# Expert stage of an attention and mixture-of-experts kernel: a three-armed Switch replaced by fp32 units of 64 tokens in nested conditions

## The chip, the cores and the metric

The kernel runs on one core of a Trainium2 chip. The metric is device time in microseconds (us). The engines are TensorE (PE in the profile; its weight loads are PEld), VectorE (DVE), ScalarE (ACT), GpSimd (POOL) and SyncE (SP), which here issues DMAs. Each engine has its own instruction stream with its own branches.

## The reference

Attention with queries pooled by two, then a top-1 mixture of experts with a fixed capacity. Shapes: 2 batches, 8 heads, 1152 positions, head dimension 64; pooled queries make N = 1152 tokens of D = 512. There are 8 experts with F = 1024 and a capacity of 288 tokens; tokens beyond the capacity are dropped and their rows stay zero.

```python
q_pool = q.reshape(B, H, S // 2, 2, 64).mean(axis=3)
attn = softmax(q_pool @ k.T / 8)
x = (attn @ v) as (1152, 512)                  # tokens
expert_idx = argmax(x @ w_gate); gate_w = its softmax probability
disp[e, pos] = x[i]                            # at most 288 tokens of each expert, in order
h = maximum(einsum('ecd,edf->ecf', disp, w1), 0)
y = einsum('ecf,efd->ecd', h, w2)
out[i] = gate_w[i] * y[expert_idx[i], pos[i]]  # 0 for dropped tokens
```

Inputs, outputs and all results are fp32. With the inputs used, the experts get 27, 61, 69, 288 (374 before the cut), 51, 63, 267 and 240 tokens.

## The kernel before

The first part computes attention and the routes of the tokens, and writes each token's row with its gate and its row numbers into a DRAM buffer `xs`, sorted by expert, 288 rows for each. `classes()` turns the counts per expert into class numbers, and each engine loads the eight class numbers into registers (L1027). Eight products that nobody reads (`warm`, L697) keep TensorE running meanwhile. The change leaves all this alone but for `classes()`.

The expert stage starts at about 350 us. For each expert in turn there is a `tc.Switch` on its class (L1039) with one arm per class, written out as straight code in each of the eight Switches. Classes are: no token, up to 32, up to 64, up to 128, up to 256, up to 288 tokens. There are three kinds of arms:

- "columns" (`by_columns`, up to 64 tokens) works in plain fp32. The tokens, transposed, are the stationary operand and the raw weights stream past in pieces of 256 columns. A group of 64 tokens fills half of TensorE's columns, so two groups stand side by side, each with its half of F. First product L834, relu on ScalarE (L841) for the first half of columns and on VectorE (L839) for the second, transposes back (`turn`, L846), copies (ScalarE L851, VectorE L849), second product L869, gate factor and copy `yo` (L799), send by an indirect DMA on GpSimd (L805).
- "tokens" (`by_tokens`, up to 128) and "weights" (`by_weights`, up to 256 or 288) split every operand into two float32r parts and add three products. The weights are split in the arm: ScalarE casts (L738) and VectorE subtracts (L740). First products are L907 and L939, second ones L917 and L975, and L961 for the last 32 tokens of 288.

In this run experts 0 to 7 take the arms for 32, 64, 128, 288, 64, 64, 288 and 256. Weights come in chunks of 1 MB, four for an expert, into eight buffers `wraw`; six chunks are loaded during attention, and a chunk that is done with starts the load of the chunk eight later. Each arm also loads the tokens of the expert after the next (SyncE), transposes the first 128 tokens of the next (`trans_x0`, L768, with its copy `xf` at L770) and splits those and the next expert's first weight chunk.

The order of instructions on SyncE, ScalarE, VectorE and TensorE is that of the text (`manual_schedule`); GpSimd's is set by the scheduler. At the end of an arm each engine leaves the Switch (rows at L1062, in which registers are set) and goes to the arm of the next one (from L1062 to L1039).

Of the kernel before, what the change touches and what calls it, by code (L numbers as in the profile page):

```python
# [23 lines left out]
NR, NR0 = 8, 6  # L24
FAR = 1.0e6
ALT = 2
# [8 lines left out]
def attention_moe(ctx: ExitStack, tc, cap, q, k, v, wg, w1, w2, out):  # L35
    nc = tc.nc
# [56 lines left out]
    NG0 = cap if cap <= 288 else 2 * P  # L93
    sizes = sorted({n for n in (D // 2, D, P, 2 * P, cap) if n <= cap})
    arms = [(-1, 0, "none")]
    for n in sizes:
        arms.append((arms[-1][1], n, "columns" if n in (D // 2, D) else "tokens" if n <= P else "weights"))
    cls_i = const.tile([P, E], I32, name="cls_i")
# [6 lines left out]
    # tokens of each expert so far on each partition: small whole numbers, exact in float32r  # L105
# [52 lines left out]
    # the small terms of the mixed tile: high parts of both heads' keys, low parts of both heads' queries  # L158
# [100 lines left out]
    def prep_first():  # L259
        # nothing runs beside the first pair's operands: split straight out of PSUM  # L260
# [136 lines left out]
    # query groups of a second product: (group of P^T, columns, token tiles and their rows)  # L397
# [134 lines left out]
    def classes():  # L532
        ps = m_ps.tile([P, 512], F32, tag="t", name="cps")
        nc.tensor.matmul(ps[:, 0:E], ones, totals[0][:, 0], start=True, stop=True)
        cl = xp.tile([P, 2, E], F32, tag="cl", name="cl")
        c, g = cl[:, 0], cl[:, 1]
        for i, (lo, _, _) in enumerate(arms[1:]):
            d = c if i == 0 else g
            nc.vector.tensor_scalar(out=d, in0=ps[:, 0:E], scalar1=lo + 0.5, scalar2=None, op0=ALU.is_ge)
            if i:  # L540
                nc.vector.tensor_tensor(out=c, in0=c, in1=g, op=ALU.add)
        return nc.vector.tensor_copy(cls_i, c)

    # filled before the tokens are placed: slots without a token hold zeros and a token beyond the last
# [49 lines left out]
    with ExitStack():  # L594
# [12 lines left out]
        # the last pair: its products, outputs and routes as soon as each group of queries is through  # L607
# [85 lines left out]
        # the tensor engine halves its clock when it idles for long: products that nobody reads keep it up  # L693
        # while the last tokens are placed
# [7 lines left out]
    # up to 64 tokens go through float32 passes in two column groups; more go through three passes of  # L702
    # operands split into two float32r parts each
    NM = NG0 + NG0 % 2
    XB = (NG0 + P - 1) // P
    N0 = min(P, NG0)
    h_p = ctx.enter_context(tc.tile_pool(name="hp", reuse_waits="tile", bufs=1))
    y_p = ctx.enter_context(tc.tile_pool(name="yp", reuse_waits="tile", bufs=2))
# [5 lines left out]

    hh = h_p.tile([P, FC, NM], F32R, name="hh")
    hl = h_p.tile([P, FC, NM], F32R, name="hl")
    hs = h_p.tile([P, 2, 512], F32, name="hs")
    ht = h_p.tile([P, 4, P], F32, name="ht")
    hr = h_p.tile([P, FC, D], F32, name="hr")
    whs = [ws_p.tile([P, 4, 512], F32R, name=f"wh{i}") for i in range(4)]  # L720
    wls = [ws_p.tile([P, 4, 512], F32R, name=f"wl{i}") for i in range(4)]
    xes = [xe_p.tile([P, XB, ROW], F32, name=f"xe{i}") for i in range(2)]
    gts = [xe_p.tile([P, XB + 3], F32, name=f"gt{i}") for i in range(4)]
    ids = [xe_p.tile([P, XB + 3], I32, name=f"id{i}") for i in range(4)]
    xfs = [xe_p.tile([P, DC, N0], F32, name=f"xf{i}") for i in range(2)]
    xhs = [xe_p.tile([P, DC, NM], F32R, name=f"xh{i}") for i in range(2)]
    xls = [xe_p.tile([P, DC, NM], F32R, name=f"xl{i}") for i in range(2)]
    wraw += [ws_p.tile([P, 4, 512], F32, name=f"wraw{i}") for i in range(NR0, NR)]
    if NM > NG0:
        for t in xhs + xls:  # L730
            nc.vector.memset(f32(t[:, :, NG0:NM]), 0.0)

    def split_w(i, a, alt=False):
        r, h, lo = wraw[i % NR], whs[i % 4], wls[i % 4]
        if alt:
            nc.vector.tensor_copy(h[:, a], r[:, a])
        else:
            nc.scalar.copy(h[:, a], r[:, a])  # L738
        eng = nc.gpsimd if alt else nc.vector
        eng.tensor_tensor(out=lo[:, a], in0=r[:, a], in1=f32(h[:, a]), op=ALU.subtract)  # L740

    def blocks(n):
        return [(s, min(P, n - s)) for s in range(0, n, P)]

    def load_x(e, o, n, b0, b1):
        for s, c in blocks(n)[b0:b1]:
            r = e * cap + o + s
            nc.sync.dma_start(out=xes[e % 2][0:c, s // P, :], in_=xs[r:r + c, :])

    def tags(e, b, c):  # L750
        xe, gt, it = xes[e % 2], gts[e % 4], ids[e % 4]
        nc.gpsimd.tensor_copy(gt[0:c, b:b + 1], xe[0:c, b, DM:DM + 1])  # L752
        nc.gpsimd.tensor_copy(it[0:c, b:b + 1], xe[0:c, b, DM + 1:DM + 2].bitcast(I32))
        if b == 0:
            sides = [(XB + i, w) for i, w in ((0, D), (2, D // 2)) if w <= c]
        else:
            sides = [(XB + 1, c)] if c in (D // 2, D) else []
        for col, w in sides:
            for g in range(2):
                rows = slice(g * w, (g + 1) * w)  # L760
                nc.gpsimd.tensor_copy(gt[rows, col:col + 1], xe[0:w, b, DM:DM + 1])
                nc.gpsimd.tensor_copy(it[rows, col:col + 1], xe[0:w, b, DM + 2 + g:DM + 3 + g].bitcast(I32))

    def trans_x0(e):
        xe, xf = xes[e % 2], xfs[e % 2]
        ps = tr_ps.tile([P, 512], F32, tag="tr", name="xps")
        for d in range(DC):
            nc.tensor.transpose(ps[:, d * N0:(d + 1) * N0], xe[0:N0, 0, d * P:(d + 1) * P], ident[0:N0, 0:N0])  # L768
        tags(e, 0, N0)
        nc.scalar.copy(xf, ps[:, 0:DC * N0].rearrange("p (d c) -> p d c", c=N0))  # L770

    def split_x0(e):
        xf, xh, xl = xfs[e % 2], xhs[e % 2], xls[e % 2]
        nc.scalar.copy(xh[:, :, 0:N0], xf)
        nc.vector.tensor_tensor(out=xl[:, :, 0:N0], in0=xf, in1=f32(xh[:, :, 0:N0]), op=ALU.subtract)

    def trans_x(e, n, first):
        xe, xh, xl = xes[e % 2], xhs[e % 2], xls[e % 2]
        bl = blocks(n)[first:]
        if not bl:  # L780
            return
        s0 = bl[0][0]
        for d in range(DC):
            ps = (h_ps if d == 3 else tr_ps).tile([P, 512], F32, tag="h" if d == 3 else "tr", name="xps")
            for s, c in bl:
                nc.tensor.transpose(ps[:, s:s + c], xe[0:c, s // P, d * P:(d + 1) * P], ident[0:c, 0:c])
            nc.scalar.copy(xh[:, d, s0:n], ps[:, s0:n])  # L787
            nc.vector.tensor_tensor(
                out=xl[:, d, s0:n], in0=ps[:, s0:n], in1=f32(xh[:, d, s0:n]), op=ALU.subtract
            )  # L790
        for s, c in bl:
            tags(e, s // P, c)

    def send(e, b, c, ps, halves=1, part=None):
        n = DM // halves
        gate = gts[e % 4][0:c, b:b + 1]
        yo = y_p.tile([P, DM], F32, tag="yo", name="yo", bufs=4)
        if part is None:
            nc.scalar.activation(yo[0:c, 0:n], ps[0:c, 0:n], AF.Copy, scale=gate)  # L799
        else:  # L800
            yq = y_p.tile([D, n], F32, tag="yq", name="yq", bufs=1)
            nc.scalar.copy(yq[0:c], ps[part:part + c, 0:n])
            nc.vector.tensor_tensor(out=yq[0:c], in0=ps[0:c, 0:n], in1=yq[0:c], op=ALU.add)
            nc.vector.tensor_scalar(out=yo[0:c, 0:n], in0=yq[0:c], scalar1=gate, scalar2=None, op0=ALU.mult)
        ins = nc.gpsimd.indirect_dma_start(  # L805
            out=out.rearrange("t (g d) -> (t g) d", g=halves),
            out_offset=bass.IndirectOffsetOnAxis(ap=ids[e % 4][0:c, b:b + 1], axis=0),
            in_=yo[0:c, 0:n],
            in_offset=None,
            bounds_check=NTOK * halves - 1,  # L810
            oob_is_err=False,
        ).ins
        tc.declare_no_dep(ins, group="send", reason="each token has a row of its own")
        tc.add_to_no_dep_group("send", ins)

    def load_next(i):
        if i + NR < 4 * E:
            load_w(i + NR)

    def by_columns(e, n, step):  # L820
        xf = xfs[e % 2]
        c0 = 4 * e
        raw = [wraw[(c0 + c) % NR] for c in range(4)]
        G = P // n
        Q = F // G // 256

        def up(q):
# [10 lines left out]
            if q:  # L838
                nc.vector.tensor_scalar_max(hs[:, q, 0:256], ps[:, 0:256], 0.0)  # L839
            else:  # L840
                nc.scalar.activation(hs[:, q, 0:256], ps[:, 0:256], AF.Relu)  # L841
# [224 lines left out]
```

## Time and profile before

| | us |
|---|---|
| median of three runs | 570.49 (569.73 to 574.44) |
| span of the profiled execution | 565.9 |
| TensorE busy in it | 468.0 (83%) |
| VectorE, ScalarE, GpSimd busy | 330.8, 296.5, 164.1 |
| mean granted TensorE clock | 0.917 of full speed |

The profiled execution has no time of its own beside its span. The span, from the first to the last instruction, is 4.6 us below the median of the runs, which also hold the start and the end around it. Times below count from the start of the span.

In the chain of waits, a piece belongs to the engine and line that ran, and "issue" is time in which an engine waited for nothing that the profile shows; names such as ACTq are an engine's sequencer with registers and branches. TensorE's fp32 products leave two records each. DMA share is the mean busy share of the core's 16 DMA engines.

### The profile page before, as it was taken

What the parts mean: (1) busy time and instruction counts of PE and PEld (TensorE: products, weight loads), DVE (VectorE), ACT (ScalarE), POOL (GpSimd) and SP (SyncE); (2) the same over time, 40 slices, a digit from 0 to 9 for tenths busy, and PEclk for the clock granted to TensorE, in tenths of its full rate; (3) what the DMA queues carried; (4) which work ended last, traced back from release to release, by engine and by line L of the source; (5) the groups of instructions that cost most, each with busy time, mean ns of one, the idle gap of its engine ahead of it and who ended that gap; (6) DMA issues with size and microseconds to landing.
All of it is one profiled execution on the core that took longest, in us unless ns stands there. A gap on an engine that the chain in (4) does not pass through costs nothing.

```text
span 565.9 us, 8678 instructions
## 1 busy us (share of the span) xinstructions
PE 468.0 (83%) x2809; PEld 328.8 (58%) x2809; DVE 330.8 (58%) x837; ACT 296.5 (52%) x840; POOL 164.1 (29%) x303
## 2 busy tenths in 40 slices
PE   4889989989989989999999987465839965569794
PEld 3657757656656656666676753233529732368693
DVE  6697886785878976876875663202637320237160
ACT  5767766657657647666766640211527330236250
POOL 4574450351442652432410012110321221011101
PEclk9799999999999989999999997767878996769898
DMA  8899932311321421320120006869745566900101
GB/s 245 188 298 374 351 91 48 83 49 43 83 75 53 120 65 38 83 46 2 43 47 1 1 37 199 273 203 314 236 147 173 178 213 192 324 18 4 45 2 38
DMA packets 56790, 71.11 MB, mean 126 GB/s; under 512 B 21794, under 2 KB 32036, under 8 KB 56608
## 3 DMA queue, kind: packets, MB, share of 16 engines
q1 hardware_dynamic: 52672, 57.72, 33.9%
q0 software_dynamic: 3392, 11.50, 5.7%
q14 instruction: 135, 1.11, 0.9%
q8 instruction: 47, 0.77, 0.6%
q10 hardware_dynamic: 544, 0.02, 0.1%
HBM read 52.48 MB, written 11.92 MB: 114 GB/s over the span
## 4 chain that ended last, share of the span: by engine, by line
PE 59%; DVE 18%; issue 15%; ACT 5%; DMA 1%; another core or an unknown queue 1%; ACTq 0%; SPq 0%; POOL 0%; POOLq 0%; DVEq 0%
PE s L346 13%; PE pv L409 13%; PE tp L384 10%; PE hps L939 8%; DVE q L243 7%; DVE negm L351 5%; PE yps L975 5%; PE warm L697 2%; PE xps L439 2%; ACT wh L738 2%; DVE pt L393 2%; PE hps L834 1%; ACT p L367 1%; PE kps L195 1%
## 5 line engine op out<-in xcount | busy, mean ns | idle before, releaser
L351 DVE TENSOR_REDUCE negm<-s 128x1 f32<-128x384 f32 x216 | 115.8, 553 | 63.6 <-PE s L346 60.4
L367 ACT ACTIVATE p<-s,negm 128x384 f32<-128x384 f32 x216 | 124.4, 582 | 38.3 <-DVE negm L355 32.8
L346 PE MATMUL s<-k,q 128*128 128x384 f32 x432 | 127.7, 387 | 9.8 <-ACT p L367 9.8
L384 PE MATMUL tp<-ident,p 128*128 128x128 f32 x648 | 108.6, 280 | 7.5 <-DVE pt L393 7.5
L409 PE MATMUL pv<-pt,vraw 128*64 128x256 f32 (+2 forms) x612 | 106.9, 406 | 0.0
L395 ACT COPY pt<-tp 128x384 f32<-128x384 f32 (+1 forms) x160 | 70.0, 453 | 50.8 <-PE tp L384 49.8
L346 PEld LDWEIGHTS s<-k,q 128*128 128x128 f32 x432 | 68.1, 195 | 48.4 <-ACT p L367 32.8
L384 PEld LDWEIGHTS tp<-ident,p 128*128 128x128 f32 x648 | 80.5, 142 | 24.2 <-DVE pt L393 11.9
L409 PEld LDWEIGHTS pv<-pt,vraw 128*64 128x64 f32 x612 | 41.8, 136 | 33.8 <-issue 19.2
L206 POOL TENSOR_TENSOR k<-kts,k 64x384 fp32r<-64x384 f32 x42 | 42.2, 1005 | 65.7 <-DVE k L205 40.4
L740 DVE TENSOR_TENSOR wl<-wraw,wh 128x512 fp32r<-128x512 f32 x78 | 50.0, 685 | 14.5 <-ACT wh L738 13.4
L249 POOL TENSOR_TENSOR q<-qts,q 64x256 fp32r<-64x256 f32 (+1 forms) x76 | 50.8, 676 | 17.2 <-DVE q L243 9.4
L738 ACT CAST wh<-wraw 128x512 fp32r<-128x512 f32 x78 | 44.0, 619 | 12.7 <-issue 12.7
L805 POOL DMA_INDIRECT out_dram<-yo,id x13 | 15.9, 1224 | 101.0 <-ACT yo L799 55.0
L393 DVE COPY pt<-tp 128x384 f32<-128x384 f32 (+1 forms) x80 | 40.2, 511 | 6.8 <-PE tp L384 6.0
L367 ACT ACTIVATION_READ_ACCUMULATOR p<-s,negm 128x1 f32 x216 | 43.8, 203 | 0.0
L243 DVE CAST q<-qts 64x256 fp32r<-64x256 f32 (+1 forms) x70 | 42.2, 617 | 1.1
L834 PE MATMUL hps<-wraw,xf 128*64 128x256 f32 (+1 forms) x128 | 20.8, 544 | 21.1 <-issue 21.1
L839 DVE TENSOR_SCALAR hs<-hps 128x256 f32<-128x256 f32 x3 | 1.3, 425 | 46.7 <-PE hps L834 46.7
L834 PEld LDWEIGHTS hps<-wraw,xf 128*64 128x64 f32 (+1 forms) x128 | 11.3, 182 | 28.8 <-issue 28.1
L939 PE MATMUL hps<-xh,wh 128*128 128x288 f32 (+1 forms) x96 | 19.4, 330 | 8.4 <-ACT xh L787 8.4
L752 POOL COPY gt<-xe 128x1 f32<-128x1 f32 (+1 forms) x13 | 2.4, 183 | 74.9 <-issue 65.3
(157 smaller groups left out, 583.9 us busy)
## 6 DMA issues: line engine op xcount, KB each, us to landing
wraw<-in_moe_w_dram SPq DMA_DIRECT2D x32, 1024.0 KB, 8.6
vraw<-in_v_dram SPq DMA_DIRECT2D x8, 576.0 KB, 4.0
kc<-k SPq DMA_DIRECT2D x16, 288.0 KB, 3.8
xs<-zrow POOLq DMA_DIRECT2D x4, 1032.0 KB, 7.0
xe<-xs SPq DMA_DIRECT2D x16, 258.0 KB, 3.6
qraw<-in_q_dram SPq DMA_DIRECT2D x16, 256.0 KB, 3.5
kraw<-in_k_dram SPq DMA_DIRECT2D x14, 288.0 KB, 4.3
out_dram<-zrow POOLq DMA_DIRECT2D x2, 1024.0 KB
```

The source lines that it names most:

```text
L243: nc.vector.tensor_copy(tl[r0, 0, c], qt_s[rs, a:z])
L249: nc.gpsimd.tensor_tensor(out=tl[r0, 1, c], in0=qt_s[rs, a:z], in1=f32(tl[rs, 0, c]), op=ALU.subtract)
L346: nc.tensor.matmul(ps[:, 0:CW], a, w, start=i == 0, stop=i == len(terms) - 1)
L351: nc.vector.tensor_reduce(out=negm3[g][:, j:j + 1], in_=ps[:, 0:CW], axis=AX.X, op=ALU.max, negate=True)
L367: nc.scalar.activation(pexp[g][:, j * CW:(j + 1) * CW], sthird.pop(n)[:, 0:CW], AF.Exp, bias=negm3[g][:, 3:4], scale=1.0, accum_out=sums[p ...
L384: nc.tensor.transpose(ps[:, i * P:(i + 1) * P], pexp[g][:, kt * P:(kt + 1) * P], ident)
L393: nc.vector.tensor_copy(dst, sr)
L395: nc.scalar.copy(dst, sr)
L409: nc.tensor.matmul(ps[j * D:(j + 1) * D, 0:n], vraw[:, j, kt, :], pts[p, j, src][:, kt, c0:c0 + n], start=kt == 0, stop=kt == KT - 1,)
L738: nc.scalar.copy(h[:, a], r[:, a])
L740: eng.tensor_tensor(out=lo[:, a], in0=r[:, a], in1=f32(h[:, a]), op=ALU.subtract)
L939: nc.tensor.matmul(ps[:, 0:ne], a[:, d, fo:fo + P], x[:, d, 0:ne], start=i == 0, stop=i == 3 * DC - 1)
```

## The change

Every expert is worked off in units: tokens 0 to 63, 64 to 127, 128 to 191, 192 to 255 in units of 64, and 256 to 287 in a unit of 32. Each unit is the "columns" arm of before, applied to its tokens. Unit 0 stands in straight code. Unit 1 stands in a condition on a flag, unit 2 in a condition inside unit 1's, and so on, so that every expert has four nested conditions. The flags (`more_i`) are loaded into registers on every engine ahead of each expert's unit 0 (L853), and each unit begins with a hint on the condition that follows. The split operands and their arms are gone. `wraw` has 16 buffers instead of eight, and the load of chunk i + 16 stands behind the nested conditions. The token buffers `xes` are three instead of two, and all blocks of an expert's tokens are transposed on TensorE and copied by ScalarE.

```diff
-NR, NR0 = 8, 6
+NR, NR0 = 16, 6
+NX = 3
...
+    units = []
+    while sum(n for _, n in units) < cap:
+        o = sum(n for _, n in units)
+        units.append((o, D // 2 if cap - o <= D // 2 else D))
+    NU = len(units)
...
-    def by_columns(e, n, step):
+    def unit(e, u, between=()):
+        o, n = units[u]
         xf = xfs[e % 2]
...
                     nc.tensor.matmul(
-                        ps[g * n:(g + 1) * n, 0:256], xf[:, d, 0:n], raw[o // 512][:, d, o % 512:o % 512 + 256],
+                        ps[g * n:(g + 1) * n, 0:256], xf[:, d, o:o + n], raw[c // 512][:, d, c % 512:c % 512 + 256],
                         start=d == 0, stop=d == DC - 1,
                     )
...
+    def later(e, u, flags):
+
+        label = f"u{e}_{u}"
+        with tc.If(flags[u - 1] > 0, preferred_fallthrough_block=True, label=label):
+            if u + 1 < NU:
+                tc.mark_branch_hint_location(f"u{e}_{u + 1}", hint=flags[u], engines=ENG)
+            nxt = units[u + 1][0] if u + 1 < NU else 0
+            unit(e, u, [lambda: trans_x(e, nxt // P)] if nxt and nxt % P == 0 else ())
+            if u + 1 < NU:
+                later(e, u + 1, flags)
...
     with tc.manual_schedule(engines=MS):
-        load_x(0, 0, NG0, 0, XB)
-        load_x(1, 0, NG0, 0, XB)
-        for i in range(NR0, NR):
+        for e in range(min(NX, E)):
+            load_x(e)
+        for i in range(NR0, min(NR, 4 * E)):
             load_w(i)
-        with tc.issue_after(routed):
-            for a in range(4):
-                split_w(0, a)
-        trans_x0(0)
-        split_x0(0)
+        trans_x(0, 0)
         for e in range(E):
-            for i in tc.Switch(cv[e], len(arms)):
-                arm(e, *arms[i][1:])
+            _, flags = nc.values_load_multi_w_load_instructions(more_i[0:1, e, :], min_val=0, max_val=1)
+            tc.mark_branch_hint_location(f"u{e}_1", hint=flags[0], engines=ENG)
+            unit(e, 0, [lambda: trans_x(e + 1, 0)] if e + 1 < E else ())
+            later(e, 1, flags)
+            if e + NX < E:
+                load_x(e + NX)
+            for i in range(4 * e + NR, min(4 * e + NR + 4, 4 * E)):
+                load_w(i)
```

On ScalarE before, expert 4's arm for 64 tokens reads as follows; L1062 is the way out of the arm, L841 the relu, L770 the copy of the next expert's tokens, L738 the casts of the next expert's first chunk:

```order
L1039 BRANCH_PREFETCH_HINT
L841 ACTIVATE hs<-hps 128x256
L851 COPY ht<-htp 128x256
L770 COPY xf_4046<-xps 128x512
L774 CAST xh_4048<-xf_4046 128x4x128
L738 CAST wh_4027<-wraw_154 128x512 x4
L799 ACTIVATE yo<-yps,gt_4037 128x256
L1062 UNCONDITIONAL_BRANCH
```

On ScalarE after, from the end of expert 4's fourth unit over its unit of 32 to the end of expert 5's unit 0 (L795 is the relu, L752 and L755 make yo, L853 loads the flags):

```order
L752 ACTIVATE yo<-yps,gt_4034 128x256
L838 COMPARE_AND_BRANCH
L795 ACTIVATE hs<-hps 128x256
L755 COPY yq<-yps 64x256
L838 UNCONDITIONAL_BRANCH x8
L853 TENSOR_LOAD more_i
L882 BRANCH_PREFETCH_HINT
L795 ACTIVATE hs<-hps 128x256
L805 COPY ht<-htp 128x256
L735 COPY xf_4032<-xps 128x4x128
L752 ACTIVATE yo<-yps,gt_4035 128x256
L838 COMPARE_AND_BRANCH
```

The casts are gone, and eight branches, two for each of the four conditions, stand between an expert's last unit and the next expert's load of flags.

On GpSimd before, the last expert's arm for 288 tokens ends with these rows (L761 and L762 copy gates and row numbers, L805 sends):

```order
L762 COPY id_4044<-xe_4036 32x1
L761 COPY gt_4040<-xe_4036 32x1
L762 COPY id_4044<-xe_4036 32x1
L805 DMA out_dram<-yo,id_4044 2304x256
L805 DMA out_dram<-yo,id_4044 1152x512 x2
L1062 UNCONDITIONAL_BRANCH
L1062 ISA
```

On GpSimd after, the last expert's unit of 32 and what follows it (L743 and L744 copy gates and row numbers, L758 sends; an ISA row here is a wait):

```order
L743 COPY gt_4037<-xe_4030 32x1
L744 COPY id_4041<-xe_4030 32x1
L758 DMA out_dram<-yo,id_4041 2304x256
L838 UNCONDITIONAL_BRANCH
L838 ISA
L838 UNCONDITIONAL_BRANCH
L758 DMA out_dram<-yo,id_4041 2304x256
L838 UNCONDITIONAL_BRANCH
L838 ISA
L838 UNCONDITIONAL_BRANCH
L758 DMA out_dram<-yo,id_4041 2304x256
L838 UNCONDITIONAL_BRANCH
```

The unit of 32 sends inside its condition; the sends of units 3, 2 and 1 stand behind it in that order, each at the end of its own condition, with branches between them.

More of the change, by code (lines that the diff above doesn't have):

```diff
@@ L91, in attention_moe @@
         )
[L93 to L98, printed above, removed]
+    units = []
[3 more added lines that the diff above has]
+    NU = len(units)
+    CT = units[-1][0] + units[-1][1]
+    more_i = const.tile([P, E, NU - 1], I32, name="more_i")
     x_ctx = ExitStack()
@@ L534, in classes @@
         nc.tensor.matmul(ps[:, 0:E], ones, totals[0][:, 0], start=True, stop=True)
[L535 to L542, printed above, removed]
+        cl = xp.tile([P, E, NU - 1], F32, name="cl")
+        for i, (o, _) in enumerate(units[1:]):
+            nc.vector.tensor_scalar(out=cl[:, :, i], in0=ps[:, 0:E], scalar1=o + 0.5, scalar2=None, op0=ALU.is_ge)
+        return nc.vector.tensor_copy(more_i, cl)
     nz = 4
@@ L729, in attention_moe @@
[L729 to L762, printed above, removed]
@@ L764, in trans_x0 @@
-    def trans_x0(e):
-        xe, xf = xes[e % 2], xfs[e % 2]
+    wraw += [ws_p.tile([P, 4, 512], F32, name=f"wraw{i}") for i in range(NR0, NR)]
+    xes = [xe_p.tile([P, XB, ROW], F32, name=f"xe{i}") for i in range(NX)]
+    xfs = [xe_p.tile([P, DC, XB * P], F32, name=f"xf{i}") for i in range(2)]
+    gts = [xe_p.tile([P, NU], F32, name=f"gt{i}") for i in range(4)]
+    ids = [xe_p.tile([P, NU], I32, name=f"id{i}") for i in range(4)]
+    blocks = [(s, min(P, cap - s)) for s in range(0, cap, P)]
@@ L766, in trans_x0, with load_x, trans_x @@
+    for t in xes:
+        if blocks[-1][1] < P and CT > cap:
+            nc.vector.memset(t[:, XB - 1], 0.0)
+    def load_x(e):
+        for s, c in blocks:
+            r = e * cap + s
+            nc.sync.dma_start(out=xes[e % NX][0:c, s // P, :], in_=xs[r:r + c, :])
+    def trans_x(e, b):
+        xe, xf = xes[e % NX], xfs[e % 2]
+        c = blocks[b][1]
         ps = tr_ps.tile([P, 512], F32, tag="tr", name="xps")
         for d in range(DC):
-            nc.tensor.transpose(ps[:, d * N0:(d + 1) * N0], xe[0:N0, 0, d * P:(d + 1) * P], ident[0:N0, 0:N0])
@@ L769, in trans_x0 @@
[L769 to L799, printed above, removed]
-        else:
[L801 to L804, printed above, removed]
+            nc.tensor.transpose(ps[:, d * c:(d + 1) * c], xe[0:c, b, d * P:(d + 1) * P], ident[0:c, 0:c])
@@ new lines, in trans_x, with tags @@
+        nc.scalar.copy(xf[:, :, b * P:b * P + c], ps[:, 0:DC * c].rearrange("p (d c) -> p d c", c=c))
+    def tags(e, u):
+        o, n = units[u]
+        xe, gt, it = xes[e % NX], gts[e % 4], ids[e % 4]
+        src, b = slice(o % P, o % P + n), o // P
+        for g in range(2):
+            rows = slice(g * n, (g + 1) * n)
+            nc.gpsimd.tensor_copy(gt[rows, u:u + 1], xe[src, b, DM:DM + 1])
+            nc.gpsimd.tensor_copy(it[rows, u:u + 1], xe[src, b, DM + 2 + g:DM + 3 + g].bitcast(I32))
@@ new lines, in send @@
+    def send(e, u, ps):
+        n = units[u][1]
+        c = 2 * n
+        gate = gts[e % 4][0:c, u:u + 1]
+        yo = y_p.tile([P, 256], F32, tag="yo", name="yo")
+        if n == D:
+            nc.scalar.activation(yo[0:c], ps[0:c, 0:256], AF.Copy, scale=gate)
+        else:
+            yq = y_p.tile([D, 256], F32, tag="yq", name="yq", bufs=1)
+            nc.scalar.copy(yq[0:c], ps[c:2 * c, 0:256])
+            nc.vector.tensor_tensor(out=yq[0:c], in0=ps[0:c, 0:256], in1=yq[0:c], op=ALU.add)
+            nc.vector.tensor_scalar(out=yo[0:c], in0=yq[0:c], scalar1=gate, scalar2=None, op0=ALU.mult)
@@ L814, in send, with step @@
         tc.add_to_no_dep_group("send", ins)
-    def load_next(i):
-        if i + NR < 4 * E:
-            load_w(i + NR)
-    def by_columns(e, n, step):
+    def unit(e, u, between=()):
+        o, n = units[u]
         xf = xfs[e % 2]
-        c0 = 4 * e
-        raw = [wraw[(c0 + c) % NR] for c in range(4)]
+        raw = [wraw[(4 * e + c) % NR] for c in range(4)]
         G = P // n
         Q = F // G // 256
+        todo = list(between)
+        def step():
+            if todo:
+                todo.pop(0)()
         def up(q):
@@ L863, in by_columns @@
         for i in range(NF):
-            for u in range(U):
-                j, g = divmod(i, 2) if U == 1 else (i % 2, 2 * u + i // 2)
+            for w in range(U):
+                j, g = divmod(i, 2) if U == 1 else (i % 2, 2 * w + i // 2)
                 r = g * (F // G) + j * P
                 for c in range(2):
-                    o = (2 * u + c) * n
+                    k = (2 * w + c) * n
                     nc.tensor.matmul(
-                        ps[o:o + n, 0:256], ht[:, j, g * n:(g + 1) * n],
+                        ps[k:k + n, 0:256], ht[:, j, g * n:(g + 1) * n],
                         raw[2 + r // 512][:, r % 512 // P, c * 256:(c + 1) * 256],
@@ L1027, in attention_moe @@
-    _, cv = nc.values_load_multi_w_load_instructions(cls_i[0:1, :], min_val=0, max_val=len(arms) - 1)
+            if i > 1:
+                step()
+        while todo:
+            step()
+        send(e, u, ps)
+    def later(e, u, flags):
[7 more added lines that the diff above has]
+                later(e, u + 1, flags)
```

180 lines of the change are left out of this document (13 added, 167 removed).

## The prediction

> **What bounds the kernel now.** I read the page first, then the chain of waits from 350 us on, a table of the expert stage cut at the experts' ends, and TensorE's order of time in one expert. The page:
>
> ```profile
> span 565.9 us, 8678 instructions
> ...
> PE 59%; DVE 18%; issue 15%; ACT 5%; DMA 1%; another core or an unknown queue 1%; ACTq 0%; SPq 0%; POOL 0%; POOLq 0%; DVEq 0%
> ...
> L805 POOL DMA_INDIRECT out_dram<-yo,id x13 | 15.9, 1224 | 101.0 <-ACT yo L799 55.0
> ```
>
> Over the span the chain is TensorE. The change touches only the stage after 350 us, and there the shares are others (the columns of the table: window and length in us, each engine's busy us, TensorE's granted clock, DMA share, GB/s):
>
> ```profile
> by line: issue 36.6%; PE hps L939 19.8%; PE yps L975 13.8%; ACT wh L738 4.1%; PE hps L834 3.3%; another core or an unknown queue 2.6%; PE xps L768 1.9%; PE hps L907 1.8%; PE yps L961 1.7%; PE yps L869 1.5%; PE yps L917 1.3%; DMA wraw<-in_mo
> ...
> 350.00:364.00 14.00, 6.49 (x72) 3.13 (x70) 3.55 (x7) 5.23 (x10) 1.42 (x10) 0.76 0.85 280
> 364.00:386.00 22.00, 13.10 (x72) 7.03 (x72) 4.45 (x10) 4.05 (x9) 2.34 (x11) 0.69 0.75 245
> 386.00:413.00 27.00, 17.36 (x62) 12.45 (x60) 12.15 (x18) 11.41 (x22) 7.54 (x13) 0.81 0.77 256
> 413.00:453.00 40.00, 30.83 (x188) 26.09 (x188) 17.44 (x35) 16.00 (x42) 7.30 (x21) 0.87 0.51 165
> 453.00:465.00 12.00, 8.97 (x72) 5.38 (x72) 3.52 (x7) 4.35 (x10) 2.39 (x11) 1.00 0.56 190
> 465.00:487.00 22.00, 12.70 (x72) 7.12 (x72) 3.93 (x8) 4.59 (x10) 2.41 (x11) 0.77 0.73 236
> 487.00:530.00 43.00, 32.06 (x188) 27.32 (x188) 15.91 (x32) 15.75 (x42) 6.78 (x21) 0.80 0.25 80
> 530.00:566.00 36.00, 24.95 (x148) 22.27 (x148) 11.42 (x24) 11.38 (x27) 3.25 (x5) 0.88 0.07 25
> sum 216.00, PE 146.46 PEld 110.79 DVE 72.37 ACT 72.77 POOL 33.44; mean PE 18.31 PEld 13.85 DVE 9.05 ACT 9.10 POOL 4.18
> ```
>
> Of 216 us TensorE works 146; the largest single item of the chain is "issue", time in which an engine waited for nothing that the profile shows. Where it lies, in order of time (start, length, what):
>
> ```profile
> 350.24 0.59 ACT xf L770
> ...
> 352.21 4.03 issue
> 356.24 3.38 PE hps L834 x32
> ...
> 386.17 5.89 issue
> 392.07 0.03 ACTq L1062
> ...
> 392.28 6.75 issue
> 399.03 0.03 ACTq L1039
> ...
> 440.91 11.34 PE yps L975 x48
> ...
> 452.39 0.37 issue
> ...
> 452.97 4.58 issue
> ...
> 470.75 7.28 issue
> 478.03 0.03 ACTq L1039
> ...
> 478.49 0.39 ACT hs L841
> ...
> 486.63 0.06 ACT yo L799
> ...
> 529.96 2.84 issue
> ...
> 559.72 0.42 POOL out_dram L805
> ```
>
> The long pieces stand just behind the last operation of an arm (L1062, the way out) and between L1062 and L1039 (the way into the next arm). So each jump to code that the engine does not hold costs ScalarE some 6 to 7 us while the DMA engines carry 236 to 256 GB/s (386.17, 392.28, 470.75), and 2.84 us at 529.96, where they are all but idle (25 GB/s). Where the last arm runs on into what stands right behind it, it costs 0.37 us (452.39). TensorE does not wait so long on the way out, but it then waits for ScalarE's relu.
>
> [...]
>
> **The change part by part.** Units run: experts 0, 1, 4, 5 one of 64; expert 2 two; 3 and 6 four and one of 32; 7 four.
>
> *Price of a unit.* Expert 4 (51 tokens) takes it already, at clock 1.00 (start, length, engine, line, idle before):
>
> ```profile
> 454.05 2.81 PE L834 MATMUL hps<-wraw,xf 128*64 128x256 f32 x24 [1.81 <-issue]
> 458.45 0.44 PE L846 MATMUL htp<-ident,hs 128*128 128x128 f32 x2 [1.58 <-ACT hs L841]
> ...
> 459.83 0.66 PE L768 MATMUL xps<-ident,xe 128*128 128x128 f32 x4
> ...
> 461.80 2.81 PE L869 MATMUL yps<-wraw,ht 128*64 128x256 f32 x24
> ```
>
> From 458.45 to 464.61 is 6.2 us, of which 0.6 are the next block's transposes; with the first 24 records (2.6 up to their last start) a unit is 8.0 us, 8.6 with transposes. Units 1 to 3 in a row: 3 x 8.0 + 2 x 0.6 = 25.2. The unit of 32 has half the records, but its relu, turn and copy stand uncovered: 5.0 (estimate, from 3.38 for its first product in expert 0 and the chain's short pieces).
>
> Against that, expert 3 took 452.3 - 424.0 = 28.2 us with float32r; now 8.6 + 25.2 + 5.0 = 38.8. Expert 6 loses the same 10.6, expert 7 (24.95 us of TensorE in its row, now 33.8) some 9. Expert 2 gains: 17.4 us become 16.6, and its waits for wh (L738) go. All splits leave ScalarE and VectorE; they lie beside TensorE, so that is worth nothing in experts 3, 6 and 7.
>
> *Entry.* Unit 0 of expert 0 needs no jump: it starts after xf, at 351 instead of 356.24. With the clock at 0.76 in that window it takes 10: its products end at 361 (before: 363.2).
>
> *One jump, unit 1 skipped.* After yo, ScalarE jumps once, where before it jumped out and in. Then it loads the flags and sets registers; the nearest rows are the load of L1027 and the arm's register steps:
>
> ```profile
> L1027 ACTq TENSOR_LOAD <-cls_i x1: 750/750/750, 350.9 to 350.9; - x1
> L1062 PEldq COMPARE_BRANCH  x16: 311/2844/7427, 349.0 to 553.2; - x16
> ```
>
> That is 0.75 + 0.4, say 1.2 us (between 0.4, if the load went out early, and 1.6). From relu to yo is 8.1 us at the lowered clock (478.49 to 486.63), 6.7 at full clock. So from the end of a unit to that of the next: 5.9 + 1.2 + 6.7 to 8.1, say 14.0 with DMA busy, and 2.9 + 1.2 + 6.7 = 11.0 with DMA idle. I take busy for experts 0 and 1 (ten chunks of 1 MB are asked for at the stage's start), idle for 4 and 5, because with 16 buffers the last chunks are asked for when expert 3 is through. TensorE's own way out is put at 0.3, the least of the second row, where the largest is 7.4.
>
> *Chained jumps.* The nested conditions end in unconditional branches, one for each level. Where all units ran there are three jumps beyond the neighbouring code, where unit 2 was skipped there are two. No row shows a jump right behind a jump. Bounds: 0.37 each, if the code is there by then, and 6.9 each under load. I take 2.8 each with DMA idle (529.96) and about 5 under load, since part of the fetch could run ahead. So expert 2 to 3: 6 + 4 + 1.2 + 8.1 = 19 (15 to 21). Expert 3 to 4, with the last four chunks in flight: 0.4 + 15 + 1.2, with TensorE's 2.6 us partly beside it and 5 more of relu to yo: 21 (10 to 27). Expert 6 to 7: 0.4 + 8.4 + 1.2 + 6.7 = 17 (10 to 24).
>
> *GpSimd's sends.* Those of units 4, 3, 2 and 1 now stand behind one another after the last unit, a branch between each two, and each takes 1.22 (L805). Before, the last one starts at 559.72 and the span ends at 565.9, so it needs some 6 to land. yo has four buffers and five users in an expert, so expert 4's yo takes over the one from which expert 3's unit 1 is sent, last of all: 1.2 + 4 x 1.22 + 3 jumps + 6. If a fetch runs on during the send before it, a jump costs 3.8: 23.5 after expert 3's products, 2.3 behind ScalarE's own 21 (0 to 6). ScalarE stands at that yo, and behind it are its jump and expert 5's relu. In expert 7 the same sum with idle DMA is 17 and costs nothing. At the end three sends are left when the last product is through: 0.7 + 2 x 1.22 + 2 jumps of 1.6 to 2.8 + 6.2 = 13 (10 to 15).
>
> *Sum.* Ends on TensorE: expert 0 361; expert 1 375; expert 2 389 and with unit 1 397.6; expert 3's unit 0 416.6, its others 441.8 and 446.8; expert 4 467.8; 5 481.1 with the 2.3; 6's unit 0 492.1, then 517.3 and 522.3; 7's unit 0 539.3, then 564.5; the end at 577.5, against 565.9. The weights don't bind: of the ten chunks asked for at 350, some 4 us each at 245 GB/s, the sixth is there by 374, the tenth by 390, and experts 2 and 3 start at 375 and 398.
>
> The profiled execution stands 4.6 us below the median of the runs (570.49); I add them: **582.1, say 582 us**, +2.0%. What can be told from no change is about 1%.
>
> In short, 13 long jumps of ScalarE become 12, the units of experts 3, 6 and 7 bring 30 us more products, and what the jumps and the entry give back is less. With chained jumps at 2.8 everywhere, experts 2 and 3 end 7 us earlier and the 2.3 are gone: 573. With the chained ones under load at 6.9, 8 us more: 590. That is the forecast's own range.
>
> **Rivals.**
> [...]
> *2. Hinted jumps arrive early on ScalarE.* Hints now stand right ahead of each unit, one way only to go. For it: TensorE's 311 ns. Against: the ways out in before were hinted as well, and ScalarE waited 5.89. The price is 5.5 us under load, three times, and 2.5 idle, twice: 21.5 less, **561**, faster. This decides where a skipped unit costs ScalarE under 1 us.
> *3. Both, so that no jump costs anything.* Experts 0 to 7 then stand at TensorE's work alone: **533**. [...]
> *4. TensorE misses too*, since a skipped unit is hinted for the way that is not gone. Then the first 24 records no longer lie beside ScalarE's wait: 2.6 to 5 us in five places, **600**. For it: 7427 ns at the most.
>
> **How the numbers follow.** Forecast 0.50 (0.14 of it within 1%, since it begins at 573 and 576.2 is the bound), rival 1 0.15, rival 2 0.16, rival 3 0.10, rival 4 0.09. Faster by over 1% are rivals 1 to 3, 0.41, less 0.03 for a half-way rival 2 near 568: 0.38. Within: 0.14 + 0.03 = 0.17. Slower: 0.36 + 0.09 = 0.45. The range leaves out rival 3 and the far half of rival 4: 548 to 600.
>
> **What would show it.** Chain of waits: after yo in experts 0 and 1, one issue piece of 5 to 7 us on ScalarE, in 4 and 5 of about 3; behind the 32-unit of expert 3 three such pieces of 3 to 6. TensorE's rows: units 8 us apart inside experts 3, 6 and 7. Sends of expert 7 about 4 us apart at the end. Wrong if the pieces behind a chain's first are under 1 us (rival 1), if ScalarE's piece after expert 0 is (rival 2), or if TensorE's first products of expert 1 start over 5 us after the last of expert 0 (rival 4).

## The result and the profile after

The changed kernel takes 553.7 us (median of four runs, 550.52 to 555.41) against 570.11 for the kernel before (569.18 to 574.44): a ratio of 0.970, 95% interval 0.964 to 0.975. The forecast was 582, slower. The time lies in the stated range (548 to 600), but on the other side of no change.

The ends of the experts on TensorE (us from the start of the span), read from its order of time in both traces (expert 7 before: from ScalarE's last yo, since some of TensorE's last records are missing):

| | before | forecast | after |
|---|---|---|---|
| expert 0 | 363.2 | 361 | 359.4 |
| expert 1 | 386.0 | 375 | 369.2 |
| expert 2 | 412.5 | 397.6 | 399.6 |
| expert 3 | 452.2 | 446.8 | 446.8 |
| expert 4 | 464.6 | 467.8 | 457.1 |
| expert 5 | 486.5 | 481.1 | 468.3 |
| expert 6 | 529.2 | 522.3 | 508.7 |
| expert 7 | 557.3 | 564.5 | 544.0 |
| end of the span | 565.9 | 577.5 | 553.0 |

The stage cut at these ends (window and length; busy us of PE, PEld, DVE, ACT, POOL; granted clock, DMA share, GB/s), after:

```profile
350.00:359.40 9.40, 8.87 (x72) 5.07 (x72) 0.85 (x2) 1.82 (x4) 1.18 (x8) 1.00 1.05 365
359.40:369.20 9.80, 8.94 (x74) 5.39 (x72) 0.85 (x2) 1.81 (x4) 0.99 (x1) 1.00 1.05 387
369.20:399.60 30.40, 22.43 (x144) 12.42 (x144) 1.70 (x4) 3.63 (x8) 3.14 (x10) 0.78 1.05 376
399.60:446.80 47.20, 39.79 (x350) 22.86 (x350) 3.82 (x9) 7.21 (x17) 5.54 (x26) 0.93 0.54 189
...
468.30:508.70 40.40, 38.22 (x350) 22.49 (x350) 3.82 (x9) 7.21 (x17) 4.35 (x18) 1.00 0.02 8
...
sum 203.00, PE 169.97 PEld 98.74 DVE 17.65 ACT 31.34 POOL 30.82; mean PE 21.25 PEld 12.34 DVE 2.21 ACT 3.92 POOL 3.85
```

TensorE is busy 170 of 203 us here, 146 of 216 before. Expert 1 now lasts 9.8 us instead of 22.8, with 8.9 us of products in it. ScalarE shows why. First its waits in the stage after, where no row is ended by "issue" (engine, line, what it waited for, us, times, longest); then its order of time over the end of expert 0 (idle before an operation in brackets):

```profile
ACT yo L752 <- PE yps L822: 58.4, 14, 6.6
ACT hs L795 <- PE hps L788: 39.4, 20, 6.5
ACT xf L735 <- PE xps L734: 32.3, 15, 9.8
...
ACT yo L752 <- POOL gt L743: 9.1, 1, 9.1
```

```profile
359.55 0.47 ACT L752 ACTIVATE yo<-yps,gt 128x256 f32<-128x256 f32 x1 [3.61 <-PEq L838]
362.33 0.38 ACT L795 ACTIVATE hs<-hps 128x256 f32<-128x256 f32 x1 [2.31 <-PE hps L788]
```

From the branch at 359.56 to the load of the next flags it takes 0.57 us, and 0.56 at experts 1, 4 and 5, and most of that is the end of its own yo (359.55 to 360.02); then ScalarE waits for TensorE, not for code. The three chained branches behind experts 3 and 6 take 0.15 us each. The page counts what was fetched, first before, then after:

```profile
q14 instruction: 135, 1.11, 0.9%
q8 instruction: 47, 0.77, 0.6%
```

```profile
q8 instruction: 34, 0.56, 0.4%
q14 instruction: 25, 0.20, 0.1%
```

Of the two queues that carry instructions, q14 brings 25 packets of some 8 KB instead of 135, and q8, with packets of 16 KB, 34 instead of 47.

What TensorE still waits for, after:

```profile
PE hps L788 <- ACTq L838: 9.5, 4, 6.2
PE xps L734 <- DMA xe<-xs: 4.7, 1, 4.7
PE hps L788 <- PEq L838: 3.3, 1, 3.3
```

TensorE's own branches (count; least, median and largest in ns), and its longest waits in order of time:

```profile
L838 PEldq COMPARE_BRANCH  x30: 65/170/4457, 357.3 to 544.8; - x30
```

```profile
372.45 5.39 PE L788 MATMUL hps<-wraw,xf 128*64 128x256 f32 x24 [3.26 <-PEq L838]
...
384.17 1.09 PE L734 MATMUL xps<-ident,xe 128*128 128x128 f32 x4 [4.71 <-DMA xe<-xs]
...
405.81 4.38 PE L788 MATMUL hps<-wraw,xf 128*64 128x256 f32 x24 [6.21 <-ACTq L838]
```

Behind the three waits TensorE's granted clock was 0.50 (372.50 to 378.00), 0.50 (384.20 to 388.00) and 0.62 (406.00 to 410.00), where it was 1.00 from 359.40 to 369.20. Of the three only the first is a jump: TensorE's own, over the four skipped units of expert 1 (its branch takes 4.46 us, in part beside its last products). The second waits for expert 3's token rows. SyncE issued them behind ten weight chunks, which held it for 22 us:

```profile
349.59 21.95 SPq L588 DMA_DIRECT2D wraw<-in_moe_w_dram  x10
373.97 1.46 SPq L727 DMA_DIRECT2D xe<-xs  x3
```

The third was ended by ScalarE's branch, but ScalarE had itself waited 9.1 us for GpSimd's copies of gates, and GpSimd for token rows until 397.07 and then for a send of its own. So a large part of what the changed kernel still lost was the order of the transfers, which no term of the prediction had. GpSimd's branches cost it little at the end: expert 7's last three sends start at 545.41, 546.70 and 547.98, 1.3 us apart, where the prediction looked for about 4.

### The profile page after: what moved, and what is told of

Its sections match the earlier page's. It is cut to its first block, busy times and chain, and to the rows that moved or that the text cites. A ratio compares the mean times of both kernels' runs of the same rounds, so it can differ in the third digit from the quotient of the medians.

```text
span 553.0 us, 9627 instructions
## 1 busy us (share of the span) xinstructions
PE 489.9 (89%) x3351; PEld 316.2 (57%) x3351; DVE 273.1 (49%) x735; ACT 252.8 (46%) x743; POOL 160.5 (29%) x290
## 5 line engine op out<-in xcount | busy, mean ns | idle before, releaser
L788 PE MATMUL hps<-wraw,xf 128*64 128x256 f32 (+1 forms) x640 | 77.8, 399 | 14.7 <-ACTq L838 9.5
L822 PE MATMUL yps<-wraw,ht 128*64 128x256 f32 (+1 forms) x640 | 75.5, 389 | 3.6 <-DVE ht L803 2.8
L793 DVE TENSOR_SCALAR hs<-hps 128x256 f32<-128x256 f32 x18 | 7.6, 424 | 133.1 <-PE hps L788 130.0
L788 PEld LDWEIGHTS hps<-wraw,xf 128*64 128x64 f32 (+1 forms) x640 | 44.4, 140 | 40.7 <-issue 12.2
L822 PEld LDWEIGHTS yps<-wraw,ht 128*64 128x64 f32 (+1 forms) x640 | 40.7, 135 | 27.7 <-issue 5.7
L758 POOL DMA_INDIRECT out_dram<-yo,id x20 | 19.5, 976 | 113.7 <-DVE yo L757 49.6
L752 ACT ACTIVATE yo<-yps,gt 128x256 f32<-128x256 f32 x18 | 8.5, 473 | 78.7 <-PE yps L822 58.4
L803 DVE COPY ht<-htp 128x256 f32<-128x256 f32 x20 | 8.5, 425 | 44.0 <-PE htp L800 41.1
```

Of the source, the lines that this page charges most:

```text
L788: nc.tensor.matmul(ps[g * n:(g + 1) * n, 0:256], xf[:, d, o:o + n], raw[c // 512][:, d, c % 512:c % 512 + 256], start=d == 0, stop=d == DC ...
L822: nc.tensor.matmul(ps[k:k + n, 0:256], ht[:, j, g * n:(g + 1) * n], raw[2 + r // 512][:, r % 512 // P, c * 256:(c + 1) * 256], start=i == ...
```

## The experiments

The theory at the start: a jump costs a fetch where its target is not in the code already fetched. In the changed kernel ScalarE's whole expert is 33 rows, so by the theory a skip stays inside; TensorE's is hundreds of instructions (expert 0 alone has 72 records of products and 72 of weight loads), so it does not. The rival: conditions with a hint and a preferred way are cheap by their form, and a Switch is dear by its form.

**Distance, on the nested conditions.** A control with one more condition, never true, inside the unit of 32, and the same with 256 instructions of code in it that are never run, the ballast:

```diff
+            else:
+                with tc.If(flags[u] > 0, preferred_fallthrough_block=True, label=f"never{e}"):
+                    for _ in range(BALLAST):              # 1 in the control, 256 in e1_ballast
+                        nc.scalar.copy(hs[0:1, 0, 0:1], hs[0:1, 0, 1:2])
```

> The changed kernel with a sixth flag that is never set and, inside the condition of the unit of 32, one more condition on it that holds a single tiny ScalarE copy, never run. It is the control for the next run. Both theories: the three experts that run all or most units (3, 6, 7) skip one more condition at about 0.2 us for each engine, so the span is 553 to 555 us and ScalarE's gaps at the skipped units of experts 0, 1, 4 and 5 stay at 0.5 to 0.7 us.

> The same, with 256 tiny ScalarE copies in the condition that is never run. Nothing more is executed, but ScalarE's code of one expert grows from 33 rows to some 290. Theory of distance (a jump costs a fetch only where its target lies outside the code already fetched, and in the changed kernel ScalarE's whole expert is so short that the target is there): ScalarE's gap between yo of a skipped unit 1 and the next expert's flags grows from 0.5 to 4 to 7 us in experts 0 and 1 (DMA busy) and to 2.5 to 4 in 4 and 5, and the skip of the never-run condition in experts 3 and 6 costs as much; the span grows by 15 to 30 us against the control, and the instruction packets of the small queue (25 in the changed kernel) rise to 50 or more. Rival theory (the form of the jump counts: nested conditions with a preferred way and a hint are cheap, a Switch is dear): the span stays within 2 us of the control.

Measured: 557.2 us (span 555.5; 553 to 555 expected) and 569.6 us (567.9), one run each: 12.4 us for code that nobody executes, a little less than the 15 to 30 expected. ScalarE, behind expert 0, in the control and then with the ballast:

```profile
359.52 0.47 ACT L754 ACTIVATE yo<-yps,gt 128x256 f32<-128x256 f32 x1 [3.61 <-PE yps L824]
363.34 0.38 ACT L797 ACTIVATE hs<-hps 128x256 f32<-128x256 f32 x1 [3.35 <-PE hps L790]
```

```profile
357.40 0.47 ACT L754 ACTIVATE yo<-yps,gt 128x256 f32<-128x256 f32 x1 [3.61 <-PE yps L824]
366.83 0.38 ACT L797 ACTIVATE hs<-hps 128x256 f32<-128x256 f32 x1 [8.96 <-PE hps L790]
```

From ScalarE's branch to the next load of flags it is 5.64 and 5.37 us at experts 0 and 1, 2.76 and 2.65 at 4 and 5 (control 0.57, 0.56, 0.56, 0.56). Counted from the end of yo that is 5.2 us at expert 0 and 2.3 at expert 4 (0.1 in the changed kernel), near the prices that the prediction had put on every jump, DMA busy and idle. Behind expert 3 the skip of the code that is never run takes 5.5 us. All eight skips of ScalarE together take some 27 us more than in the control. The total is smaller because TensorE has skips of its own at the same places. Its waits ahead of its first products, in the control and then with the ballast:

```profile
PE hps L790 <- issue: 10.3, 4, 4.0
```

```profile
PE hps L790 <- ACTq L840: 25.6, 5, 8.7
```

In the control TensorE stands four times for its own skip and the load of the flags behind it. With the ballast it stands at the same four places until ScalarE's branch is through (5.75, 5.48, 2.87 and 2.76 us), so its next products do not run beside ScalarE's jump there; the fifth wait, 8.7 us ahead of expert 3, is 7.9 in the control. Only behind experts 3 and 6 do TensorE's first 24 records run beside the jump, in full or in part. Only ScalarE's code grew, and only q14's packets rise, from 29 in the control to 43 (50 or more expected; q8 stays at 34), so q14 brings ScalarE's code. That the target lies in the code already fetched in the control and outside it with the ballast is read from these times and packets, not seen. So for nested conditions distance decides (0.57 us against 5.64 at expert 0), and the form alone does not make them cheap.

**Hints.** Both calls of `mark_branch_hint_location` and the labels are left out.

```diff
-            tc.mark_branch_hint_location(f"u{e}_1", hint=flags[0], engines=ENG)
...
-            if u + 1 < NU:
-                tc.mark_branch_hint_location(f"u{e}_{u + 1}", hint=flags[u], engines=ENG)
```

> The changed kernel without any of its branch hints. Theory of distance: ScalarE, VectorE, GpSimd and SyncE jump as before at 0.5 to 0.7 us, since their targets are there anyway; only TensorE, whose skip passes four units, can lose, from 2.0, 4.5, 2.4 and 0.4 us in experts 0, 1, 4, 5 to at most 5 each: 0 to 10 us more. Rival (the hints made the jumps cheap on ScalarE): gaps of 3 to 6 us on ScalarE in experts 0, 1, 4, 5 and the chain of expert 2, 15 to 25 us more.

Measured: 560.3 us, ratio to before 0.984 (0.977 to 0.991); 6.6 us more than the changed kernel. ScalarE's branches stay at 0.56 us. TensorE's, from branch to load of flags, go from 2.35, 4.67, 2.56 and 2.35 us at experts 0, 1, 4 and 5 to 6.31, 7.87, 6.06 and 3.79 (part of these is the wait for its own last products); in expert 2, where unit 2 is skipped, its branch goes from 0.35 to 6.35 us. So the hints are worth some 7 us, and of these two engines only TensorE's skips change.

**No conditions at all.** Units by the known counts, as straight code:

```diff
-        with tc.If(flags[u - 1] > 0, preferred_fallthrough_block=True, label=label):
+        if u < (1, 1, 2, 5, 1, 1, 5, 4)[e]:
```

> The changed kernel without conditions: each expert's units that this input needs, as straight code (the choice by the token count is left out). It prices what the conditions still cost. Theory: TensorE's skips (2.0, 4.5, 2.3, 2.4, 0.4 us) with the halved clock after them, ScalarE's 0.5 to 0.7, GpSimd's sends behind the conditions and the chain of branches go, but the wait of 4.7 us for expert 3's token rows stays: 528 to 541 us. If the conditions are free: 550 to 555.

Measured: 536.9 us (ratio 0.943, 0.934 to 0.952), 16.8 us below the changed kernel: the price left of its conditions. In this trace TensorE has one long wait, and it is not a jump:

```profile
383.98 1.09 PE L734 MATMUL xps<-ident,xe 128*128 128x128 f32 x4 [11.29 <-DMA xe<-xs]
```

**The Switch of the kernel before.** It has six arms, one for each class, of three kinds. First the kernel before as straight code, then with a small Switch of three arms at experts 0, 1, 4 and 5 only:

```diff
-            for i in tc.Switch(cv[e], len(arms)):
-                arm(e, *arms[i][1:])
+            arm(e, *arms[(1, 2, 3, 5, 2, 2, 5, 4)[e]][1:])       # e3_before_straight
```

```diff
+            if e in (0, 1, 4, 5):                                # e5_small_switch
+                for i in tc.Switch(cv[e], 3):
+                    arm(e, *arms[i][1:])
+            else:
+                arm(e, *arms[{2: 3, 3: 5, 6: 5, 7: 4}[e]][1:])
```

> The kernel before without its Switch: each expert has only the arm that this input takes, as straight code (the choice by the class is left out). It prices all jumps of the kernel before. Theory: the 13 long pieces of issue on ScalarE in the chain (74 us in all) go, and some 15 us of that was hidden beside TensorE's first products; waits for casts appear in part of the rest: 500 to 515 us. If the jumps lay beside other work: 550 or more.

> The kernel before, where experts 0, 1, 4 and 5 keep a Switch, but one of three arms (no token, up to 32, up to 64), and the others stand in straight code as in the run above. ScalarE's code of such a Switch is some 25 rows instead of some 100. Theory of distance: ScalarE's ways into and out of these arms take 0.5 to 1 us instead of 5 to 7, so the kernel is 3 to 15 us above the one with straight code, what is left being TensorE's. Rival (a Switch is dear by its form, nested conditions are not): eight jumps of 5 to 7 us under load, 30 us or more above it.

Measured, one run each: 494.3 us (span 492.6) for straight code, where 500 to 515 was expected: the eight Switches cost some 77 us beside 571.8 for the kernel before run next to it. With four small Switches 524.4 (span 522.6): 30.1 us more, just where the rival begins. ScalarE's code of such a Switch is some 25 rows, and yet its way into expert 0's arm takes 6.0 us (352.27 to 358.25) and the way out 4.4 (366.36, the end of its last copy, to 370.73). The ways into the other three take 6.0, 2.8 and 6.1; the ways out of those, where the last arm ran, under 0.5 us behind the branch. TensorE, in this run:

```profile
358.52 3.45 PE L834 MATMUL hps<-wraw,xf 128*32 128x256 f32 x32 [7.99 <-issue]
...
376.50 5.39 PE L834 MATMUL hps<-wraw,xf 128*64 128x256 f32 x24 [11.03 <-issue]
```

These two waits are TensorE's own ways in (branches of 7.40 us at 350.85 and 8.01 at 368.21), longer than ScalarE's beside them. So the 30.1 us are not ScalarE's price alone, and the total decides little; what decides are ScalarE's rows, long although its code is short. q14 carried 20 packets in the straight run, 70 in this one. So distance in rows does not explain a Switch: here the theory fell, and for the Switch the rival held.

**Token rows.** SyncE's order at the start of the stage, then GpSimd's copies:

```diff
-NX = 3
+NX = 8
...
-        for e in range(min(NX, E)):
+        for e in range(3):
             load_x(e)
-        for i in range(NR0, min(NR, 4 * E)):
+        for i in range(NR0, NR):
             load_w(i)
+            if i % 2 and 3 + (i - NR0) // 2 < E:
+                load_x(3 + (i - NR0) // 2)
...
-        tags(e, u)                       # e7_x_tags alone
+        if not u:
+            for w in range(NU):
+                tags(e, w)
```

> The changed kernel with eight token buffers instead of three; SyncE issues the token rows of experts 3 to 7 between the ten weight chunks at the start of the stage, instead of behind them and behind each expert's conditions. Theory: TensorE's wait of 4.7 us for expert 3's rows at 379.5, the halved clock behind it, and GpSimd's late tags and sends go; of the gap of 6.2 us ahead of expert 3 only that part goes which is not the landing of expert 2's own send: 6 to 14 us less than the changed kernel, 540 to 548. If the order on SyncE is not the cause: 552 to 556.

> The same, and GpSimd copies the gates and row numbers of all five units of an expert in unit 0 instead of each in its own condition, so that no copy stands behind the landing of a send. Theory: the wait of ScalarE's yo for GpSimd's copy (9.1 us in expert 2, of which TensorE lost 6.2 and the halved clock after it) goes as well: 2 to 8 us less than the run before, 534 to 544. If the copies are not the cause: as the run before.

Measured: 540.8 us (ratio 0.948, 0.939 to 0.957) and 542.8 (0.949, 0.939 to 0.960). The order on SyncE, with the five more buffers that it needs (the two are not separated), is worth 12.9 us; the copies, with that order in place, nothing. In the first, TensorE waits 1.25 us ahead of expert 3 instead of 6.21, and nowhere for token rows. So GpSimd's lateness was the lateness of the rows passed on, and the part of it that I had put on the landing of a send was not to be seen any more.

> Both edits at once: the changed kernel's units as straight code for this input (the choice by the token count is left out), and eight token buffers with SyncE's token rows issued between the weight chunks. It closes the sum of the unit's price: nothing but TensorE's own work and its entry and end are left. Theory: the wait of some 10 us ahead of expert 2 in the straight run goes: 522 to 530 us. The prediction's third rival put this case at 533. If the weight chunks themselves come too late: 535 or more.

Both edits at once: 525.7 us (span 524.0). This is the units' own price: 28 us below the changed kernel, of which the order on SyncE alone gives 12.9 and the conditions alone 16.8; they add up but for 1.7 us.

**Conditions with the arms of before.** Two arms, 64 columns or float32r for 288, in two hinted conditions, first with the loads inside the arms as before, then behind them:

```diff
-            for i in tc.Switch(cv[e], len(arms)):
-                arm(e, *arms[i][1:])
+            tc.mark_branch_hint_location(f"big{e}", hint=cv[e], engines=ENG)
+            with tc.If(cv[E + e] > 0, preferred_fallthrough_block=True, label=f"small{e}"):
+                arm(e, *arms[2][1:])
+            with tc.If(cv[e] > 0, preferred_fallthrough_block=True, label=f"big{e}"):
+                if e + 1 < E:
+                    tc.mark_branch_hint_location(f"small{e + 1}", hint=cv[E + e + 1], engines=ENG)
+                arm(e, *arms[5][1:])
+            if e + 2 < E:                                        # f3_loads_out alone, and out of the arms
+                load_x(e + 2, 0, NG0, 0, XB)
+            for i in range(4 * e + NR, min(4 * e + NR + 4, 4 * E)):
+                load_w(i)
```

> The kernel before with its Switch replaced by two conditions in a row for each expert, each with a hint: up to 64 tokens run the arm for 64 columns, all others the float32r arm for 288 (expert 2 with 69 tokens too, some 11 us more than its own arm). Theory: what was dear is the Switch's way into an arm and out of it on every engine, not its arms. ScalarE's jumps pass some 7 or 30 rows and take 0.5 to 1 us; TensorE's pass 150 to 400 instructions and take 2 to 6 us each, eight of them. From 494 for straight code: + 11 + 20 to 35 = 525 to 540 us. If long arms are dear in any form: 555 or more.

> As f2_two_arms, but the loads of token rows and of weight chunks stand behind each expert's two conditions instead of inside the arms. Theory: TensorE's long waits in f2_two_arms (13.8, 6.6 and 5.3 us, ended by SyncE's sequencer at the conditions) come from SyncE, which at a condition it skips first waits for its own outstanding transfers, and with the loads outside they go: 26 us less, of which some 10 come back because chunks are asked for only at an expert's end, and eight buffers hold two experts: 535 to 545 us. If SyncE's waits are not the cause: 550 to 560, as before the edit.

Measured: 556.0 us (ratio 0.968, 0.960 to 0.976), then 526.6 (0.919, 0.915 to 0.923). The first misses the 525 to 540 expected and meets the number named for long arms that are dear in any form, but the trace gives another reason. In f2_two_arms ScalarE's branches take 0.1 to 0.7 us but for one of 2.7, and TensorE stands elsewhere:

```profile
375.79 1.11 PE L765 MATMUL xps<-ident,xe 128*128 128x128 f32 x4 [6.60 <-SPq L1039]
396.33 2.63 PE L783 MATMUL xps<-ident,xe 128*128 128x128 f32 x8 [13.82 <-SPq L1037]
...
479.19 1.11 PE L765 MATMUL xps<-ident,xe 128*128 128x128 f32 x4 [5.32 <-SPq L1039]
```

The trace shows what SyncE waited for there. Behind the branch at 363.99 that skips the second condition (L1039), its rows pass at 370.39, 373.06 and 375.65, each within 0.02 us of the last landing of one of the three weight chunks that it had issued at 357.86, 361.62 and 362.10; TensorE's transposes start at 375.79. With the loads outside these waits are gone, and the longest is TensorE's own jump ahead of expert 2:

```profile
373.58 2.63 PE L783 MATMUL xps<-ident,xe 128*128 128x128 f32 x8 [6.33 <-PEq L1034]
```

The result, 29 us less, is better than the expected 535 to 545: that chunks are asked for later cost nothing visible. f3_loads_out beats both kernels, 27 us below the changed one.

> The same two arms and the same loads behind them as in f3_loads_out, but the choice is a Switch of two arms for each expert instead of two hinted conditions. ScalarE's code of an expert is some 45 rows in both. Theory: a Switch sends each engine to an arm, and behind it, by jumps whose targets are not in the code fetched, however short the arms are; ScalarE takes 3 to 7 us for the way in, and as much for the way out of the first arm: 40 to 65 us more than f3_loads_out, 565 to 590, and the small instruction queue carries over 60 packets instead of 29. Rival (what was dear in the kernel before was the number of its arms, or the loads inside them): within 10 us of f3_loads_out.

The last run takes f3_loads_out and puts the two conditions back into a Switch of two arms:

```diff
+            for i in tc.Switch(cv[e], 2):
+                arm(e, *arms[(2, 5)[i]][1:])
```

Measured: 573.0 us (span 571.3; one run), 46 more than f3_loads_out with the same arms and loads, as expected. ScalarE's waits in the stage, the same of f3_loads_out, and the page's line on the packets of g1_switch_two:

```profile
ACT xh L784 <- issue: 22.6, 2, 11.4
ACT hs L837 <- issue: 22.2, 2, 11.6
ACT yo L796 <- issue: 16.4, 7, 3.9
```

```profile
ACT yo L796 <- issue: 13.1, 5, 3.8
ACT hs L837 <- issue: 2.5, 1, 2.5
```

```profile
q14 instruction: 111, 0.91, 0.6%
```

What the Switch adds are the waits of xh and hs; that of yo is nearly the same in both. Behind eleven of its sixteen branches in the stage ScalarE stands 3.3 to 6.2 us; the first way in and the four ways out of the last arm take under 0.5. In f3_loads_out only one takes over 1 us, 2.6, and 29 packets were fetched on that queue. The conditions have a hint on the way in and the Switch has not, but e2_nohint lost only 6.6 us without its hints, and none on ScalarE. So it was neither the number of arms nor the loads in them, but the Switch. Why most of its jumps are that long, however short the arms, is not shown.

## Why the prediction was wrong

- **The step that failed** is *one jump, unit 1 skipped*, and with it *chained jumps*: "One jump, unit 1 skipped. After yo, ScalarE jumps once" was priced at 5.9 us busy and 2.9 idle, the rows of the Switch. Measured 0.56 from the branch, 0.1 from the end of yo. The rows were right for a Switch and were carried over to another construct; the ballast shows that they would nearly have held, 5.2 and 2.3 us from the end of yo, had ScalarE's skip been 256 instructions longer. I had taken every condition's end for fresh code, and the arms of the Switch too. What spoke against it was at hand and not used: ScalarE's expert is 33 rows after and some 100 before, and the order shows it. The number of rows alone would not have settled it, though: the small Switch has some 25 and is dear. The other terms of the same step: the load of the flags with its registers was put at 1.2 us and took 0.4 (360.13 to 360.55), and TensorE's own way out was put at 0.3, where its branches took 1.97, 4.46, 2.35 and 0.35 us at experts 0, 1, 4 and 5.
- **Rivals.** The result is nearest to the third (no jump costs anything, neither the first behind yo nor those chained behind it) on every engine but TensorE: its price of 533 lies between the 536.9 of the straight run, which still waits for expert 3's rows, and the 525.7 of the one that does not, and what parts 533 from 553.7 is not jumps on ScalarE but TensorE's own and the transfers. The first rival (only the chained jumps free, 0.37 us each: 554) agrees with the measured time, but by chance: it would have left 5.9 us at experts 0 and 1. The second had the right place and the wrong cause: without hints ScalarE's jumps stay as cheap. The fourth happened in small: with the hints TensorE's worst branch took 4.46 us, and of that TensorE lost 3.3 ahead of expert 2, not 2.6 to 5 in five places; its sign, over 5 us ahead of expert 1, was 0.85.
- **Chained jumps**: 5 us under load and 2.8 with DMA idle forecast, 0.15 measured. The 5 rests on part of a fetch that runs ahead, which no run shows. Expert 3 to 4 was put at 21 us and took 10.3, 6 to 7 at 17 and took 10.3.
- **Price of a unit**: right. Units 1 to 3 of expert 3 take 25.1 us (416.3 to 441.4; forecast 25.2); the unit of 32 takes 5.4 (forecast 5.0). Experts 3 and 6 did lose TensorE's time: 39.8 and 38.2 us busy, 30.8 and 32.1 before.
- **Entry**: right in kind. Unit 0 starts at 350.5 and its clock was 1.00, not 0.76: 359.4 instead of 361.
- **The weights don't bind**: right for the chunks and wrong for what stands behind them. I had counted the ten chunks' landing but not that SyncE is held by them until 371.5, so the rows of expert 3 are issued at 373.97. The sum did not have that these rows now stand behind the chunks in SyncE's queue; undoing it is worth 12.9 us. By chance it hid the error on the jumps: up to the end of expert 3 forecast and trace agree to the tenth, 446.8.
- **GpSimd's sends**: the 2.3 us at expert 4 did not appear. No run shows the term that it rests on, 3.8 us for a jump whose fetch runs on during the send before it; behind expert 3 the four sends start at 448.91, 450.14, 451.43 and 452.71, 1.2 to 1.3 us from one to the next with the send of 0.92 to 0.98 in it. A wait of ScalarE's yo for GpSimd came in expert 2 instead, 9.1 us, and by another way. The end was put at 13 after the last product and took 9.0.
- **The 4.6 us between profile and median**: after, they are 0.7. Every run listed is 1.7 us longer than its own span (554.7 against 553.0); the rest is that the profiled execution of before was shorter than the median and that of after longer. Some 4 of the 28 us of error are this.

## What to carry to other kernels

Before a jump is priced, ask how much of its engine's code it passes: here a ScalarE skip of one 33-row expert cost 0.56 us and the same skip with 256 more instructions up to 5.6. Where between the two the border lies was not measured, and the jumps of a Switch were dear over fewer rows (6.0 us in and 4.4 out over some 25). A two-armed Switch cost 46 us more in eight uses than two hinted conditions with the same arms. Keep DMA issues out of conditional code, and issue small transfers that someone waits for ahead of large ones: here these two were worth 29 and 13 us.

## What was not expected of the hardware

The Switch's jumps were dear although its ScalarE code was some 25 rows (6.0 us in, 4.4 out). Code that is never run cost 12.4 us by its length alone. Hints helped TensorE (6.31 us without, 2.35 with them at expert 0) and made no difference on ScalarE (0.56 us in both). Issuing a 1 MB load held SyncE for up to 6.0 us (362.88 to 368.89) while earlier ones were in flight, and a skipped condition with loads in it held SyncE until its own earlier loads had landed (363.99 to 375.65 in f2_two_arms), with TensorE behind it.
